# Two small cuts in a TensorE-bound transformer kernel: a PSUM tile of their own for four transposes, and smaller last pieces

## Chip, cores and metric

One core of one Trainium2 chip. The metric is the time of one execution in device microseconds. The span of a profile, from its first to its last instruction, is shorter than the time of the same execution: by about 1.7 us in 51 of the 60 executions for which both are known, by 1.9 to 2.9 us in the other nine. Figures with three decimals are starts or lengths of single instructions in the packed traces, called the records below; the views merge and round them.

## The reference

Four layers follow each other on x of 2048 tokens by 1024 features in bf16, twice this pair:

```python
x = x + A(layernorm(x))   # sliding dilated attention, 32 heads of 32, window 8, step 2; wqkv, wo
x = x + B(layernorm(x))   # gated MLP: (relu(x @ W_gate) * (x @ W_up)) @ W_down, 3584 hidden features
```

Nearly all of the work is matrix products. The kernel treats the tokens in blocks of 512, each of four tiles of 128 tokens.

## The kernel before

Only the first few microseconds and the last few matter here. All matmuls go through one helper (line 132), all VectorE (DVE) work of the first blocks through another (line 106), so in the profile the instructions are told apart by their tiles. PSUM is the memory in which the matmuls of this kernel leave their results, SBUF the one to which VectorE and ScalarE bring them; a bank of PSUM holds 512 fp32 columns here. `psum` is a pool of six one-bank accumulators, `psum_l` one tile of two banks.

The start: tile 0 of the tokens is normalised, transposed on TensorE (PE) and copied out of PSUM. Its projections on the value weights begin, and tile 1 follows with its transposes in two portions of four.

```python
def turn(t, halves=(0, 1)):
    ...
    elif t == 0:
        tps[t] = [psum.tile([P, KC // 2, P], BF16, tag="acc", name=f"tp{h}")[:] for h in range(2)]
    else:
        both = psum_l.tile([P, 2, KC, P], BF16, tag="L", name="tp_pair")
        tps[t] = [both[:, h, 0:KC // 2, :] for h in range(2)]
    for c in (h * (KC // 2) + i for h in halves for i in range(KC // 2)):
        with pe_group():
            tail_pe[0] = nc.tensor.transpose(tps[t][c // (KC // 2)][:, c % (KC // 2), :],
                                             xna[:, t, c * P:(c + 1) * P], ident[:]).ins
...
def second(h):
    turn(1, (h,))          # four transposes of tile 1
    copy(1, "v", h)        # PSUM -> SBUF on DVE, 512 columns
    ...
def head():
    for kc in range(KC // 2):
        for c in range(KC):
            if (kc, c) == (KC // 2 - 1, KC // 2):
                ln["second"](0)
            prod(kc, c, 0, 1)              # projections of tile 0, 128 columns each
    ln["second"](1)
# next on PE: prod(kc, c, 1, 2), tile 1's projections from the first copy
```

The end: the down projection of the last block of tokens, in two halves of 512 output columns. Each half sums 28 hidden chunks into accumulators, one for each piece of a tile, adds x on DVE, and stores.

```python
def cols_of(half):
    cols = [(t, 0, SLAB) for t in range(TPB)]
    if n == NN - 1 and half == 1:
        cols[-1:] = [(TPB - 1, 0, SLAB // 2), (TPB - 1, SLAB // 2, SLAB)]
    return cols
...
pair = psum_l.tile([P, TPB // 2, BLK], F32, tag="L", name="dacc_pair")
own = {2: pair[:, 0, :], 3: pair[:, 1, :]} if len(cols) == TPB else {2: pair[:, 0, :]}
accs[half] = [own[i] if i in own else psum.tile([P, BLK], F32, tag="acc", name=f"dacc{i}")[:]
              for i in range(len(cols))]
...
for a, (t, c0, c1) in zip(accs[half], cols):       # for each of four slabs of hidden chunks
    for jl in range(nfc):
        mm(a[:, c0:c1], lhsT=hT[:, j, t * P:(t + 1) * P], rhs=wsl[:, jl, c0:c1], ...)
...
for a, (t, c0, c1) in zip(accs[half], cols_of(half)):
    xs = x_tiles[b * TPB + t][:, half * SLAB + c0:half * SLAB + c1]
    run(nc.vector.tensor_tensor, xs, a[:, c0:c1], xs, op=ALU.add)
    ...  # store xs, on the SP or the ACT queue
```

## Time and profile before

The first three runs took 1617.74, 1617.75 and 1618.02 us.

The page of the profiled run: busy time by engine, then the chain of work that ended last.

```profile
span 1616.1 us, 18879 instructions
...
PE 1607.6 (99%) x7584; PEld 786.4 (49%) x7633; DVE 1138.5 (70%) x962; ACT 473.5 (29%) x964; POOL 180.3 (11%) x168
...
PE 99%; issue 0%; DMA 0%; DVE 0%; POOL 0%; ACT 0%; DVEq 0%
PE acc_u L132 24%; PE acc_g L132 24%; PE dacc L132 18%; PE acc_v L132 7%; PE acc_k L132 7%; PE acc_q L132 7%; PE acc_wo L132 7%; PE dacc_pair L132 6%; DMA x<-in_A_x_dram 0%; PE tp_pair L384 0%; DVE bst L103 0%; DVE bst L106 0%; POOL rstd L3
```

PE is busy for 99% of the span, and the chain is PE. The table of waits of PE over the whole program has three rows:

```profile
engine line waited for: us in total, times, longest us
PE scratch L132 <- DVE ones L309: 1.5, 1, 1.5
PE tp L384 <- DVE xn_first L106: 0.8, 1, 0.8
PE tp_pair L384 <- DVE xnT_first L106: 0.3, 1, 0.3
```

The first two are the start. The third is the one that the change aims at. The chain of waits around it (start, length, what; "issue" is time in which nothing is seen to be waited for):

```profile
8.99 0.28 PE acc_v L132 x5
9.27 0.36 PE tp_pair L384 x4
9.63 0.02 issue
9.66 0.44 DVE xnT_first L106
10.09 0.04 issue
10.13 0.38 PE tp_pair L384 x4
10.52 0.39 PE acc_v L132 x7
```

Four transposes of tile 1 are followed by the DVE copy of their result, then by the other four transposes, then by projections. In between PE has four projections of tile 0 (9.46 to 9.68 us), which are not on the chain. The second four transposes read nothing that the copy writes and write another bank. They wait because both portions lie in one tile, `tp_pair`, and the built program waits by tile.

The DVE timeline of the last microseconds (start, length, engine, line, operation, tiles, shape, count, and what ended the idle time before):

```profile
1610.45 0.69 DVE L838 TENSOR_TENSOR x<-dacc,x 128x512 bf16<-128x512 f32 x1 [20.95 <-PE dacc L132]
1611.31 0.69 DVE L838 TENSOR_TENSOR x<-dacc,x 128x512 bf16<-128x512 f32 x1 [0.17 <-PE dacc L132]
1612.18 0.69 DVE L838 TENSOR_TENSOR x<-dacc_pair,x 128x512 bf16<-128x512 f32 x1 [0.17 <-PE dacc_pair L132]
1612.78 0.74 DVE L838 TENSOR_TENSOR x<-dacc,x 128x256 bf16<-128x256 f32 x2
```

The adds of tiles 0 and 1 start 0.04 us after the last matmul of their accumulator. So does that of tile 2, at 1612.18. The two adds of tile 3 then follow in a row, at 1612.78 and, in the instruction's own record, 1613.115. The last store is issued at 1613.554 and the span ends 2.58 us after that.

### The profile page before, as it was taken

To read this page: it belongs to the slowest core of one execution; us is meant where nothing else is said; L and a number is where in the kernel's file an instruction comes from. 1 tells how busy PE (TensorE), PEld (TensorE's weight loads), DVE (VectorE), ACT (ScalarE), POOL (GpSimd) and SP (SyncE) were. 2 spreads that over 40 slices of the span, in tenths; PEclk is the share of its full clock that TensorE was granted. 3 is DMA by queue.
4 is the path that set the end of the run, shared out by engine and by line. 5 is a ranking of instruction groups with operands and counts; after the bars stand their busy time and mean duration, and the time that the engine had idled before them with its cause. 6 is when DMAs were issued, how large, how long until landed. Compare 5 with 4: busy or idle time off the path is not lost.

```text
span 1616.1 us, 18879 instructions
## 1 busy us (share of the span) xinstructions
PE 1607.6 (99%) x7584; PEld 786.4 (49%) x7633; DVE 1138.5 (70%) x962; ACT 473.5 (29%) x964; POOL 180.3 (11%) x168
## 2 busy tenths in 40 slices
PE   9999999999999999999999999999999999999999
PEld 6646544444444445444454444544445444444444
DVE  5999989996989698929389293893939939311211
ACT  4753312132115313603136031361313311131110
POOL 3400100010003002300053000530005100000000
PEclk9999999999999999999999999999999999999999
DMA  9767857596669666784747847489575884655452
GB/s 308 181 187 247 219 163 255 183 218 203 208 195 227 191 185 208 194 248 145 227 159 203 237 156 226 156 202 255 163 227 155 207 241 157 209 161 177 156 167 67
DMA packets 359064, 317.92 MB, mean 197 GB/s; under 512 B 105024, under 2 KB 332736, under 8 KB 358464
## 3 DMA queue, kind: packets, MB, share of 16 engines
q1 hardware_dynamic: 358272, 315.87, 67.1%
q8 instruction: 59, 0.97, 0.3%
q10 hardware_dynamic: 704, 0.85, 0.2%
q14 instruction: 29, 0.24, 0.0%
HBM read 266.29 MB, written 34.66 MB: 186 GB/s over the span
## 4 chain that ended last, share of the span: by engine, by line
PE 99%; issue 0%; DMA 0%; DVE 0%; POOL 0%; ACT 0%; DVEq 0%
PE acc_u L132 24%; PE acc_g L132 24%; PE dacc L132 18%; PE acc_v L132 7%; PE acc_k L132 7%; PE acc_q L132 7%; PE acc_wo L132 7%; PE dacc_pair L132 6%; DMA x<-in_A_x_dram 0%; PE tp_pair L384 0%; DVE bst L103 0%; DVE bst L106 0%; POOL rstd L327 0%; PE L L132 0%; DVE x L838 0%
## 5 line engine op out<-in xcount | busy, mean ns | idle before, releaser
L132 PE MATMUL acc_u<-xnT_b,w_u 128*128 128x512 bf16 x1792 | 423.3, 379 | 0.0
L132 PE MATMUL acc_g<-xnT_b,w_g 128*128 128x512 bf16 x1792 | 423.3, 379 | 0.0
L791 ACT ACTIVATE r<-acc_g 128x512 bf16<-128x512 f32 x224 | 133.6, 596 | 727.5 <-PE acc_g L132 696.8
L106 DVE TENSOR_TENSOR hT<-acc_u,r 128x512 bf16<-128x512 f32 x224 | 150.6, 685 | 241.2 <-PE acc_u L132 238.5
L132 PE MATMUL dacc<-w_d,hT 128*128 128x512 bf16 (+1 forms) x1372 | 300.4, 375 | 1.5
L132 PEld LDWEIGHTS <-hT 128*128 128x128 bf16 x1820 | 178.0, 98 | 209.0
L132 PEld LDWEIGHTS <-w_u 128*128 128x128 bf16 x1792 | 175.3, 98 | 211.4
L132 PEld LDWEIGHTS <-w_g 128*128 128x128 bf16 x1792 | 175.4, 98 | 211.4
L106 DVE TENSOR_TENSOR pv<-a,vhm 128x4096 bf16<-128x4096 bf16 x64 | 143.5, 2282 | 0.0
L838 DVE TENSOR_TENSOR x<-dacc,x 128x512 bf16<-128x512 f32 (+1 forms) x38 | 24.5, 672 | 154.2 <-PE dacc L132 154.2
L606 DVE TENSOR_TENSOR t<-q,k 128x2048 f32<-128x2048 bf16 x56 | 128.0, 2292 | 6.7 <-ACT k L541 4.6
L106 DVE TENSOR_TENSOR t<-q,k 128x2048 f32<-128x2048 bf16 x56 | 127.4, 2285 | 3.7 <-ACT k L541 2.6
L106 DVE TENSOR_TENSOR pv<-pv 128x1024 bf16<-128x1024 bf16 (+1 forms) x128 | 113.7, 949 | 0.0
L547 POOL COPY kh<-k 128x14 bf16<-128x14 bf16 x40 | 56.0, 1406 | 504.2 <-ACT k L541 504.2
L132 PE MATMUL acc_wo<-w_o,oT 128*128 128x512 bf16 x498 | 111.1, 379 | 0.7
L622 DVE TENSOR_TENSOR ac<-ac,t 128x2048 f32<-128x2048 f32 x48 | 109.6, 2284 | 0.3
L106 DVE TENSOR_TENSOR ac<-ac,t 128x2048 f32<-128x2048 f32 x48 | 109.6, 2283 | 0.0
L263 POOL TENSOR_TENSOR st_b<-st_b,neg_half 128x1 f32<-128x1 f32 x29 | 43.9, 1521 | 525.8 <-ACT st_b L262 525.8
L132 PE MATMUL dacc_pair<-w_d,hT 128*128 128x512 bf16 x413 | 95.5, 379 | 0.4
L132 PEld LDWEIGHTS <-oT 128*128 128x128 bf16 x512 | 50.2, 98 | 60.3
L258 ACT ACTIVATE xn_b<-x 128x1024 bf16<-128x1024 bf16 x29 | 30.3, 1045 | 129.3 <-DVE x L106 67.1
L444 ACT CAST vT<-acc_v 128x512 bf16<-128x512 f32 x56 | 32.6, 585 | 57.0 <-PE acc_v L132 56.1
(134 smaller groups left out, 1227.2 us busy)
## 6 DMA issues: line engine op xcount, KB each, us to landing
w_g<-in_B_W_gate_dram SPq DMA_DIRECT2D x56, 1024.0 KB, 7.1
w_u<-in_B_W_up_dram SPq DMA_DIRECT2D x56, 1024.0 KB, 5.4
w_d<-in_B_W_down_dram SPq DMA_DIRECT2D x48, 1024.0 KB, 5.9
w_o<-in_A_wo_dram SPq DMA_DIRECT2D x16, 1024.0 KB, 8.2
vhm<-v_d SPq DMA_DIRECT2D x32, 284.0 KB, 6.7
v_d<-vT SPq DMA_DIRECT2D x8, 1024.0 KB, 9.7
oT<-o_d SPq DMA_DIRECT2D x32, 256.0 KB, 3.4
w_d<-in_B_W_down_dram SPq DMA_DIRECT2D x16, 512.0 KB, 3.9
```

Source lines behind the costliest of these rows:

```text
L106: tail_dve[0] = f(*args, **kwargs).ins
L132: tail_pe[0] = nc.tensor.matmul(*args, **kwargs).ins
L258: nc.scalar.activation(xn, xt[:], ACT.Square, accum_out=sq)
L263: nc.gpsimd.tensor_tensor(rstd, vpe, neg_half[:, 0:1], op=ALU.pow)
L444: tail_act[0] = nc.scalar.copy(st["vT"][:, c, :], acc[:]).ins
L547: nc.gpsimd.tensor_copy(khalo[n][:, c, :], k[:, BLK:BLK + HALO])
L606: nc.vector.tensor_tensor(t[:], i0, i1, op=ALU.mult)
L622: nc.vector.tensor_tensor(o, i0, i1, op=ALU.add)
L791: tail_act[0] = nc.scalar.activation(rs[j][:], acc[:], ACT.Relu).ins
L838: run = dv if n < NB - 2 else (lambda f, *args, **kwargs: f(*args, **kwargs))
```

## The change

Intent: (1) let the second four transposes of tile 1 run during the copy, in a PSUM tile of their own; (2) let the last add and so the last store start earlier, by ending in smaller pieces: tile 2 in two pieces of 256 columns, tile 3 in 256, 128 and 128, with as many stores, of the same sizes, as before.

```diff
                 tps[t] = [both[:, h, 0:KC // 2, :] for h in range(2)]
+                if t == 1:
+                    tps[t][1] = psum.tile([P, KC // 2, P], BF16, tag="acc", name="tp_second")[:]
...
-                cols[-1:] = [(TPB - 1, 0, SLAB // 2), (TPB - 1, SLAB // 2, SLAB)]
+                cuts = [(TPB - 2, 0, 2), (TPB - 2, 2, 4), (TPB - 1, 0, 2), (TPB - 1, 2, 3), (TPB - 1, 3, 4)]
+                cols[-2:] = [(t, c0 * SLAB // 4, c1 * SLAB // 4) for t, c0, c1 in cuts]
...
-                        own = {2: pair[:, 0, :], 3: pair[:, 1, :]} if len(cols) == TPB else {2: pair[:, 0, :]}
+                        own = {2: pair[:, 0, :], 3: pair[:, 1, :]}
... (stores: tile 2 whole after its second piece; tile 3's first 256 columns, then its last 256 after the third piece)
```

With seven pieces, entries 2 and 3 of `own` are now the two pieces of tile 2.

## The prediction

> What bounds the kernel. The page gives TensorE (PE) 1607.6 of a 1616.1 us span, 99%, and the chain of waits is PE from end to end. The table of waits shows only three for PE: the first matmul on a memset (1.5 us), tile 0's transposes on the normalised x (0.8) and, at 10.1 us, tile 1's second four transposes on the VectorE (DVE) copy of the first four (0.3). After that PE never waits, so what is won at 10 us reaches the end, unless a load that is now just in time becomes late. What follows the last matmul (adds, last store, closing barrier) is the other exposed part.
>
> Head. In the timeline the four matmuls after the first transposes end their issue at 9.68; the second transposes start at 10.135, when the copy (9.656, 0.425 long) is done; the next projection matmul starts at 10.355. With a PSUM tile of their own the transposes run in that gap. But the projection matmul reads what the copy writes, so it now waits for the same copy and starts near 10.135. Gain: the four transposes, 4 x 55 ns = 0.22 us, and not the whole gap of 0.46. Loads have room: the second half of the value weights lands at about 10.1 and 11.5 us and is wanted from about 11.9. The extra buffer taken in the accumulator ring costs no wait that I can find.
>
> Tail, PE. Spacing in the trace: 512 columns 216 ns, 256 columns 109, 128 columns 56. Halving a matmul costs about 2.5 ns each time (the Trainium skill, "TensorE: Matmul & The Clock Gate", section "Wait — 56ns, not 53.3ns?", gives about 2.5 ns fixed per matmul; the trace agrees). Tile 2 is split once and tile 3 once more, for each of 28 hidden chunks: 56 x 2.5 = +0.14 us on PE.
>
> Tail, DVE. Before: the add of tile 2 (512 columns) starts at 1612.18, 0.04 after its last matmul; the next add follows 0.61 later, the last 0.33 after that, and takes 0.41; the last store is issued at 1613.55. The last two adds were already limited by DVE: the last piece's matmuls were done at 1613.01, its add began at 1613.115.
> After: both halves of tile 2 lie in one two-bank tile, and in the built program the first half's add waits for the last matmul of the second (the second add has no wait). So that split starts nothing earlier. DVE then runs in a row 256, 256, 256, 128, 128 columns: 3 x 0.33 + 0.20 (estimate: 0.33 less 128 columns at 1.08 ns, from 0.61 against 0.33 for 256 fewer) + 0.28 = 1.47 us, against 0.61 + 0.33 + 0.41 = 1.35.
>
> Sum at the last store's issue: -0.22 (head) + 0.13 (PE up to tile 2's end) + 0.12 (DVE) = +0.03 us. The number, queues and sizes of stores are the same, the last is still 64 KB, so landing (1.6 us) stays.
>
> Predicted: 1617.75 us, 1617.35 to 1618.15 (three runs of before already spread over 0.28). Faster by over 2%: 0.005; within 2%: 0.99; slower by over 2%: 0.005.
>
> What would show it. Head right: PE's wait at tile 1's transposes goes, a wait of the first tile-1 projection matmul for the copy appears, and that matmul starts 0.2 to 0.25 earlier. Tail right: the five adds run back to back from tile 2's last matmul, none of tile 2 starts before it, and the last store is issued within 0.1 us of 1613.55. Wrong if tile 2's first add starts about 0.44 earlier (then some 0.2 us are won), if 128-column matmuls cost more than 60 ns behind hidden-state weight loads (then a loss), or if the early gain is swallowed by a load before 25 us.

## The result

| | median | range | runs |
|---|---|---|---|
| before | 1618.12 | 1617.74 to 1618.83 | 6 |
| after | 1618.03 | 1617.73 to 1618.55 | 6 |

The ratio is 0.9999, interval 0.9986 to 1.0012. Here and below a ratio is the recorded one, from the fast runs of both kernels and with its 95% interval; it is not quite the ratio of the medians quoted. Executions over 1.5% slower than the fastest of the same kernel are left out of the means. The result is "the same", inside the predicted range.

The profiled run of after happened to be the slowest of its six:

```profile
span 1616.8 us, 19042 instructions
...
PE 1610.6 (100%) x7689; PEld 789.5 (49%) x7689; DVE 1138.9 (70%) x964; ACT 473.4 (29%) x964; POOL 180.5 (11%) x168
...
PE 99%; DMA 1%; DVE 0%; ACT 0%; issue 0%; POOL 0%; DVEq 0%; SPq 0%; ACTq 0%
PE acc_u L132 24%; PE acc_g L132 24%; PE dacc L132 18%; PE acc_v L132 7%; PE acc_q L132 7%; PE acc_wo L132 7%; PE acc_k L132 6%; PE dacc_pair L132 6%; DMA w_o<-in_A_wo_dram 1%; DMA x<-in_A_x_dram 0%; PE tp_pair L386 0%; DVE x L848 0%; DVE b
```

Its table of waits of PE:

```profile
engine line waited for: us in total, times, longest us
PE scratch L132 <- DVE ones L309: 1.5, 1, 1.5
PE tp L386 <- DVE xn_first L106: 0.6, 1, 0.6
PE acc_wo L132 <- DMA w_o<-in_A_wo_dram: 0.6, 1, 0.6
```

The wait at tile 1's transposes is gone, as intended. But a new one of 0.6 us stands in the output projection, `acc_wo` on the weights `w_o`. The chain around the former wait:

```profile
9.00 0.17 PE acc_v L132 x3
9.16 0.37 PE tp_pair L386 x4
9.53 0.02 issue
9.55 0.43 DVE xnT_first L106
9.99 0.04 issue
10.03 0.89 PE acc_v L132 x13
```

The chain now goes from the copy straight to the projections; the second transposes run beside it (from 9.58). PE is still held by the copy. The end, on DVE:

```profile
1611.01 0.69 DVE L848 TENSOR_TENSOR x<-dacc,x 128x512 bf16<-128x512 f32 x1 [21.07 <-PE dacc L132]
1611.87 0.69 DVE L848 TENSOR_TENSOR x<-dacc,x 128x512 bf16<-128x512 f32 x1 [0.17 <-PE dacc L132]
1612.74 0.76 DVE L848 TENSOR_TENSOR x<-dacc_pair,x 128x256 bf16<-128x256 f32 x2 [0.18 <-PE dacc_pair L132]
1613.42 0.81 DVE L848 TENSOR_TENSOR x<-dacc,x 128x256 bf16<-128x256 f32 x3
```

The add of tile 2 is now two adds in a row ("x2" at 1612.74). The first starts 0.87 us after the add of tile 1, as the single add did before, so the cut has started nothing earlier. Five adds run back to back where three did.

To take the run's luck out, I cut each trace at instructions that every version has, and use starts of single instructions:

- *start*: from the beginning to the first DVE copy of tile 1 out of PSUM,
- *head*: from there to the first query matmul,
- *middle*: from there to the first add of the last block's first half,
- *tail*: from there to the issue of the last store,
- *close*: from there to the end of the span.

| us | start | head | middle | tail | close | span |
|---|---|---|---|---|---|---|
| before | 9.66 | 13.939 | 1562.621 | 27.338 | 2.58 | 1616.13 |
| after | 9.55 | 13.714 | 1563.386 | 27.602 | 2.58 | 1616.83 |
| after minus before | -0.10 | -0.225 | +0.765 | +0.264 | 0.00 | +0.70 |

The change touches head and tail: -0.225 + 0.264 = +0.039 us, where the prediction had +0.03. The rest of the +0.70 is in stretches whose instructions are the same in both. The middle contains one gap in the matmuls that before has not, 0.755 us at 161.1 us, in front of `acc_wo` (0.971 from one start to the next, where the others are 0.216 apart). The experiments must tell whether the change brings that gap.

### The profile page after: what moved, and what is told of

The parts are those of the page before. It is cut to its first block, busy times and chain, and to the rows that moved or that the text cites. A ratio compares the mean times of both kernels' runs of the same rounds, so it can differ in the third digit from the quotient of the medians.

```text
span 1616.8 us, 19042 instructions
## 1 busy us (share of the span) xinstructions
PE 1610.6 (100%) x7689; PEld 789.5 (49%) x7689; DVE 1138.9 (70%) x964; ACT 473.4 (29%) x964; POOL 180.5 (11%) x168
## 4 chain that ended last, share of the span: by engine, by line
PE 99%; DMA 1%; DVE 0%; ACT 0%; issue 0%; POOL 0%; DVEq 0%; SPq 0%; ACTq 0%
PE acc_u L132 24%; PE acc_g L132 24%; PE dacc L132 18%; PE acc_v L132 7%; PE acc_q L132 7%; PE acc_wo L132 7%; PE acc_k L132 6%; PE dacc_pair L132 6%; DMA w_o<-in_A_wo_dram 1%; DMA x<-in_A_x_dram 0%; PE tp_pair L386 0%; DVE x L848 0%; DVE bst L103 0%; DVE bst L106 0%; ACT kst L540 0%
## 5 line engine op out<-in xcount | busy, mean ns | idle before, releaser
L132 PE MATMUL dacc<-w_d,hT 128*128 128x512 bf16 (+2 forms) x1428 | 302.0, 371 | 0.0
L132 PEld LDWEIGHTS <-hT 128*128 128x128 bf16 x1876 | 181.3, 98 | 206.0
L848 DVE TENSOR_TENSOR x<-dacc,x 128x512 bf16<-128x512 f32 (+2 forms) x39 | 24.5, 659 | 154.3 <-PE dacc L132 154.3
L132 PE MATMUL dacc_pair<-w_d,hT 128*128 128x512 bf16 (+1 forms) x448 | 95.9, 366 | 0.0
```

Source lines behind the costliest of these rows:

```text
L132: tail_pe[0] = nc.tensor.matmul(*args, **kwargs).ins
L848: run = dv if n < NB - 2 else (lambda f, *args, **kwargs: f(*args, **kwargs))
```

## The experiments

My theory: head and tail each do what was predicted and cancel; the gap of the middle is a load that came late by chance. The rivals: the earlier head makes the load late and so pays for itself there; and for the tail, that VectorE's number of adds matters whatever they wait for. Eight kernels were run; all gave correct results. The first four ran on one chip and share its nine runs of before (median 1617.82), the other four on another (median 1618.21).

| us | start | head | middle | tail | span | median (range; runs) |
|---|---|---|---|---|---|---|
| e1 head only | 9.74 | 13.713 | 1562.621 | 27.339 | 1616.00 | 1617.60 (1617.42 to 1617.94; 5) |
| e2 tail only | 9.96 | 13.938 | 1562.619 | 27.596 | 1616.69 | 1618.15 (1617.94 to 1618.58; 5) |
| e3 own tiles | 9.60 | 13.715 | 1562.620 | 27.373 | 1615.89 | 1617.57 (1617.48 to 1618.01; 5) |
| e4 late gate load | 9.44 | 13.938 | 1562.620 | 27.341 | 1615.91 | 1617.95 (1617.62 to 1618.85; 5) |
| e5 split copy | 9.54 | 13.582 | 1562.620 | 27.340 | 1615.67 | 1617.39 (1617.35 to 1618.95; 5) |
| e6 thin down | 9.92 | 13.937 | 1575.129 | 28.182 | 1629.71 | 1631.26 (1630.93 to 1631.60; 4) |
| e7 fine adds | 9.84 | 13.938 | 1562.620 | 28.175 | 1617.21 | 1619.68 (one run) |
| e8 change again | 9.47 | 13.715 | 1562.619 | 27.598 | 1616.00 | 1618.18 (1617.72 to 1618.30; 5) |

The record also has the span of every execution. Their means on the first chip are 1616.07 for before, 1615.92 for e1, 1616.52 for e2, 1615.94 for e3 and 1616.10 for e4; on the second 1616.43 for before, 1615.76 for e5 and 1616.38 for e8. They lean the way of the traces, but the start alone varies from 9.44 to 9.96 us in these profiles, so five runs do not fix a size.

### e1: only the transposes

```diff
+                if t == 1:
+                    tps[t][1] = psum.tile([P, KC // 2, P], BF16, tag="acc", name="tp_second")[:]
```

> Only the first half of the change: tile 1's second transposes in a PSUM tile of their own; the tail as before. Stretches read from the traces: first copy of tile 1 to first query matmul (head), first query matmul to the first add of the last block's first half (middle), that add to the issue of the last store (tail). Before they are 13.94, 1562.62 and 27.34 us, after 13.71, 1563.39 and 27.60. Theory (the two halves of the change cancel: head -0.22, tail +0.26; the 0.76 us of the middle is one late load of the output-projection weights that has nothing to do with the change): head 13.71, tail 27.34, and the middle 1562.6 plus whatever that load costs in this execution, so timed 0.2 us faster than before if enough executions are averaged. Rival (starting the matmuls earlier makes that load late, so the head gain is paid back there): middle 1563.0 or more here too, and no gain in time.

Measured: head 13.713, middle 1562.621, tail 27.339. The median is 1617.60 against 1617.82, ratio 0.9998 (0.9984 to 1.0012). The head gain is 0.226 us and all of it reaches the end: the projections start as much earlier as in after, but the middle has no gap. The rival falls for this execution. The difference of the medians, 0.22 us, has the expected size, but the interval of the ratio is far wider than that, so the times do not establish it.

### e2: only the tail

```diff
-                cols[-1:] = [(TPB - 1, 0, SLAB // 2), (TPB - 1, SLAB // 2, SLAB)]
+                cuts = [(TPB - 2, 0, 2), (TPB - 2, 2, 4), (TPB - 1, 0, 2), (TPB - 1, 2, 3), (TPB - 1, 3, 4)]
+                cols[-2:] = [(t, c0 * SLAB // 4, c1 * SLAB // 4) for t, c0, c1 in cuts]
... (own and the stores as in the change)
```

> Only the second half of the change: the tail cut as in the change, tile 1's transposes as before. Theory: head 13.94, tail 27.60 (0.14 of the 0.26 us on TensorE, 56 extra matmul starts of 2.5 ns; 0.12 on VectorE, three adds of 256 and two of 128 columns in a row where there were 512, 256, 256); timed about 0.25 us slower than before, at the edge of what five rounds can show. Rival for the late load (the head's earlier start causes it): here the head is not early, so no stall in the middle: 1562.6. Under the theory of chance the stall can appear here too.

Measured: head 13.938, tail 27.596, ratio 1.0002 (0.9989 to 1.0014), median 1618.15 against 1617.82. Within the tail, the add of tile 2 starts 26.089 us after the stretch's beginning (25.960 before, so PE costs 0.13 us up to there), and from that start to the last store are 1.507 us (1.378 before, so DVE costs 0.13 us). So by the traces this half of the change is a loss of 0.26 us, and it hides the gain of the other. (How the 0.26 us splits is tried in e3, e6 and e7.)

### e3: tile 2's pieces in accumulators of their own

```diff
-                        own = {2: pair[:, 0, :], 3: pair[:, 1, :]}
+                        own = {2: pair[:, 0, :], 3: pair[:, 1, :]} if len(cols) == TPB else {6: pair[:, 0, :]}
```

> The change, but tile 2's two halves in accumulators of their own instead of the two halves of one two-bank tile (the last 128 columns of tile 3 get the two-bank tile). Theory (the first half's add waits for the second half's matmuls because they share a tile, so the cut of tile 2 buys nothing): here tile 2's first add starts when the add of tile 1 lets it, about 0.61 us after that add started instead of 0.87; the last add is then limited by TensorE again and not by a row of adds, and the tail is 27.37 (27.35 to 27.42) instead of 27.60. Rival (VectorE is limited by the number of adds whatever they wait for): tail stays 27.55 or more.

Measured: tail 27.373 against 27.60. The DVE timeline:

```profile
1610.28 0.69 DVE L848 TENSOR_TENSOR x<-dacc,x 128x512 bf16<-128x512 f32 x1 [21.07 <-PE dacc L132]
1611.15 1.93 DVE L848 TENSOR_TENSOR x<-dacc,x 128x512 bf16<-128x512 f32 x5 [0.17 <-PE dacc L132]
1613.00 0.28 DVE L848 TENSOR_TENSOR x<-dacc_pair,x 128x128 bf16<-128x128 f32 x1
```

Five adds now follow the one of tile 1 in a row from 1611.15: tile 1 whole, two of tile 2, the first two of tile 3. In the records tile 2's first add starts 0.607 us after tile 1's, as soon as DVE is free, where it started 0.87 us after it in the change. The tail falls by 0.23 us though pieces, adds and stores are the same in number and size: so the wait of tile 2's first add for the matmuls of the second, through the shared two-bank tile, is what lost that time. The rival falls. Yet the tail is only back at the level of before (27.34): the cuts cost PE 0.14 us (the modelled end of the last matmul is 26.935 us into the tail, in before 26.796), so even with separate tiles this cut wins nothing; other cuts were not tried. One detail of the expectation is wrong: the last add is not limited by PE. It starts 0.13 us after the end of its matmuls, at the end of a row of three adds; it is the first add of that row, tile 3's first piece, that waits for PE (0.037 us after its last matmul). Times: median 1617.57 against 1617.82, ratio 0.9998 (0.9986 to 1.0011).

### e4: another load moved away from the late one

```diff
-            events.append((ends[i - RING] + 0.3 if i >= RING else 0.1 * i, lambda ...: load_slab(key, src)))
+            at = ends[i - RING] + 0.3 if i >= RING else 0.1 * i
+            at = t_wo0 + 4.0 if key == ("g", 0, 0) else at
+            events.append((at, lambda ...: load_slab(key, src)))
```

> The kernel before with one load moved: the first 1 MB of gate weights, issued at about 152 us although it is first read at 190, is issued some 12 us later, after the output-projection weights that are read from 160 us on. Theory (those two loads and the query and key stores share the queues, and the output-projection load, 8.6 us to landing before and 10.1 after, is sometimes too late): it lands in 6 us or less, no stall of the output projection in any execution, middle 1562.6, and the spread of the times of this kernel is smaller than that of the kernel before (1617.74 to 1618.83), near its low end: 1617.7 to 1617.9. Rival (the spread comes from elsewhere, or the stall is a matter of when the load is issued): median and spread as before.

The DMA issues between 142 and 158 us (out<-in, queue, count, size, us from issue to landing) of before, of after, and of e4:

```profile
w_o<-in_A_wo_dram SPq DMA_DIRECT2D x1, 1024.0 KB, 8.6
w_g<-in_B_W_gate_dram SPq DMA_DIRECT2D x1, 1024.0 KB, 10.8
```

```profile
w_o<-in_A_wo_dram SPq DMA_DIRECT2D x1, 1024.0 KB, 10.1
w_g<-in_B_W_gate_dram SPq DMA_DIRECT2D x1, 1024.0 KB, 12.2
```

```profile
w_o<-in_A_wo_dram SPq DMA_DIRECT2D x1, 1024.0 KB, 9.2
```

My expectation failed. Without the gate weights behind it the load took 9.2 us, longer than in before, and the times spread as before (1617.62 to 1618.85 against 1617.55 to 1618.48; the spans, which leave out the 2.55 us by which the 1618.85 exceeds its own, 1615.9 to 1616.3 against 1615.8 to 1616.6). So moving that load did not bring this one in early. That it has no part in the delay is not shown: with it gone, the stores of the keys (`k_d`) were issued from 152.70 us on and not from 157.27, so other transfers took its place. What the ten profiles do show is the margin. In before the load is issued at 151.29 us and the matmul that reads it starts about 9.4 us later; in after, the issue is at 150.97 us and, without the stop, the reader would have started 9.4 us later too: the change moves both alike, so it does not shorten the time that the load has. The load took 7.5, 7.9, 8.4, 8.5, 8.6, 8.7, 8.8, 8.9 and 9.2 us in nine profiles, and 10.1 in the profile of after, where PE stopped. Why it takes 7.5 us once and 10.1 another time stays open.

### e5: the copy cut in two

```diff
... (tile 1's second transposes in a tile of their own, as in e1)
-            copy(1, "v", h)
-            if h == 0:
-                return
+            if h == 0:
+                copy(1, "v", h, 0, KC // 4)
+                copy(1, "v", h, KC // 4, KC // 2)
+                return
+            copy(1, "v", h)
... (first_half, for t == 1: for kc outside, for c inside; tail as before)
```

> The head of the change, the tail of before, and the first copy of tile 1 cut in two of 256 columns, with tile 1's first projections ordered so that the first eight need only the first piece. In e1 the projections still wait for the whole copy: TensorE has nothing to do from 9.80 to 10.03 us in the profile of after. Theory (what is left of the gap is the copy's length, 0.43 us, less the transposes): the first piece takes about 0.29 us, the projections start about 0.15 us earlier and find the second piece done; head 13.55 (13.50 to 13.62) against 13.71 in e1 and 13.94 before, middle 1562.62, tail 27.34; about 0.4 us faster than before in time. Rival (another wait, the transposes themselves or the second piece, ends at the same time): head 13.68 or more.

Measured: head 13.582. The chain of waits:

```profile
9.15 0.35 PE tp_pair L386 x4
9.51 0.22 PE acc_v L132 x4
9.73 0.22 PE tp_second L386 x4
9.95 0.99 PE acc_v L132 x16
```

In this view the chain goes from PE to PE, but it counts with modelled ends of matmuls, which overlap. The records say more. The last of the transposes starts at 9.732, so at their spacing of 0.056 us the projections could have followed at 9.79. The first piece of the copy takes 0.292 us from 9.542, and the projections start at 9.887, 0.345 us after the copy's start (0.478 in after). That is 0.053 us after the end of the first piece, and in after they start 0.053 us after the end of the whole copy: PE still waits for the copy, only for a shorter one. So of the 0.233 us that the change had left on the table in the head, shortening the copy wins 0.133, and 0.10 remain behind its first piece. Head gain against before: 0.357 us; middle and tail are unchanged, so all of it reaches the end. Four of its five runs lie at 1617.35 to 1617.43, below all nine of before, and one at 1618.95 (its span is 1616.1, so 2.85 us lie outside it, where the other four have 1.7); ratio 0.9996 (0.9984 to 1.0009). By the traces it is the best version tried; by the times it is not shown to be faster.

### e6: all down matmuls cut to 128 columns

```diff
-                            mm(a[:, c0:c1], lhsT=hT[:, j, t * P:(t + 1) * P], rhs=wsl[:, jl, c0:c1],
-                               start=(j == 0), stop=(j == FC - 1))
+                            for m0 in range(c0, c1, P):
+                                mm(a[:, m0:m0 + P], lhsT=hT[:, j, t * P:(t + 1) * P], rhs=wsl[:, jl, m0:m0 + P],
+                                   start=(j == 0 and m0 == c0), stop=(j == FC - 1 and m0 + P == c1),
+                                   skip_group_check=True)
```

> The kernel before with every matmul of the down projections cut into four of 128 columns in the same accumulator (adds and stores as before): 1792 matmuls become 7168. It enlarges the one suspected cost of the tail's TensorE part. Theory (a cut costs the fixed 2.5 ns per matmul and nothing else, also with a weight load per 128 columns): 7.4 ns per former 512-column matmul, +13 us, 1630 to 1632. Rival (the Trainium skill, TensorE: Matmul & The Clock Gate, section Back-to-back issue gap, gives about 81 ns for 128 columns in a stream of weight loads and matmuls): 108 ns per former matmul, +190 us.

Measured: 1631.26 us, ratio 1.0080 (1.0064 to 1.0095). Middle and tail together grow by 12.51 + 0.84 = 13.35 us. The groups of matmuls by shape (busy time, mean ns of one, idle before):

```profile
L132 PE MATMUL dacc<-w_d,hT 128*128 128x128 bf16 x5488 | 312.1, 219 | 0.0
L132 PE MATMUL dacc_pair<-w_d,hT 128*128 128x128 bf16 x1680 | 99.0, 219 | 0.0
```

13.35 us over 1792 former matmuls of 512 columns is 7.45 ns for each, so (216 + 7.45) / 4 = 55.9 ns for one of 128 columns, with a weight load in front of each (28 of the 1792 were in two pieces already, which changes little); the records have 55 or 56 ns from start to start. The theory stands, and the cost of a cut on PE is measured enlarged: about 2.5 ns. (The lengths of single matmuls in the fence, 219 ns, overlap; it is their spacing that counts.)

### e7: the same adds in 16 pieces

```diff
-                    run(nc.vector.tensor_tensor, xs, a[:, c0:c1], xs, op=ALU.add)
+                    step = 64 if n == NN - 1 and half == 1 and t >= 2 else SLAB
+                    for m0 in range(0, c1 - c0, step):
+                        m1 = min(m0 + step, c1 - c0)
+                        run(nc.vector.tensor_tensor, xs[:, m0:m1], a[:, c0 + m0:c0 + m1], xs[:, m0:m1], op=ALU.add)
```

> The kernel before with the last three adds (512, 256, 256 columns) done in 16 adds of 64 columns, the matmuls and stores as before. It enlarges the suspected VectorE part of the tail. Theory (an add costs a fixed 0.06 to 0.07 us besides its columns, and the row of adds after tile 2's last matmul is what the last store waits for): 13 more adds, +0.8 us; tail 28.15 (28.05 to 28.3) against 27.34. Rival (only columns count, or the last store waits for TensorE): tail under 27.6.

Measured: tail 28.175 against 27.338, +0.837 us for 13 more adds, 0.064 us each. The DVE timeline:

```profile
1611.49 0.69 DVE L838 TENSOR_TENSOR x<-dacc,x 128x512 bf16<-128x512 f32 x1 [0.17 <-PE dacc L132]
1612.35 1.14 DVE L838 TENSOR_TENSOR x<-dacc_pair,x 128x64 bf16<-128x64 f32 x8 [0.17 <-PE dacc_pair L132]
1613.41 1.13 DVE L838 TENSOR_TENSOR x<-dacc,x 128x64 bf16<-128x64 f32 x8
```

From 1612.35 to the end DVE does nothing but adds, 0.131 us from one start to the next. All of their cost is in the tail, so the last store does wait for the row of adds, and not for PE.

### e8: the change once more

The edit is the whole change.

> The change once more, for a second profile of it. Theory (the stall of 0.76 us in the output projection was one late load by chance, as it came in one of six profiles so far and not in e1 and e3, which start as early): head 13.71, middle 1562.62, tail 27.60, span about 1616.1 to 1616.4; timed within 0.2 us of before. Rival (head and tail together bring the stall): middle 1563.3 again.

Measured: head 13.715, middle 1562.619, tail 27.598, span 1616.00; median 1618.18 against 1618.21, ratio 0.9999 (0.9986 to 1.0011). The gap of the middle did not come back. It appeared in one of the two profiles of the change and in none of the eight of the other versions, before among them; e1, e3 and e5 are as early and have none. The early head is therefore not sufficient for it. That it would never happen to the kernel before is not shown.

## Why the prediction was right

- *PE bounds the kernel and never waits after the first 10 us.* Right for every trace but one. The middle is 1562.619 to 1562.621 us in eight of the nine profiles whose middle has the same matmuls; in the first profile of after PE waited once more, 0.755 us, for a load. The prediction named a late load as a risk, but placed it before 25 us and blamed the early start; the run-to-run spread of a load with 0.2 to 1.9 us to spare was not seen.
- *Head, -0.22 us: the four transposes, not the whole gap.* Measured -0.225 (after), -0.226 (e1), -0.224 (e8). The projection matmuls wait for the same copy; e5 shortens that wait to half of the copy and gets 0.13 us more.
- *Tail on PE, +0.13 us up to tile 2's end.* Measured +0.131 (26.091 against 25.960). The step rests on the Trainium skill, "TensorE: Matmul & The Clock Gate", section "Wait — 56ns, not 53.3ns?", about 2.5 ns fixed for each matmul; this agrees: 216, 109 and 56 ns from start to start for 512, 256 and 128 columns, and 2.5 ns for each cut in e6.
- *Tail on DVE, +0.12 us: the cut of tile 2 starts nothing earlier.* Measured +0.133. e3 shows the reason given: with separate tiles the first add starts 0.61 us after tile 1's and not 0.87. The Trainium skill, "PSUM — Partial Sum Buffer", section "PSUM bank collisions raise a hardware error", asks for guards by bank and quadrant; the two pieces lie in two banks, and e3 gives correct results without that wait, so the wait came from the tile and not from the memory.
- *Sum +0.03 us.* Measured +0.039 in the first profile, +0.036 in e8. The times cannot confirm it: the range of 0.4 us to either side would have held as well if neither half had done anything. That the sum is right for the reasons given is read from the stretches and from e1, e2 and e3.
- *One sign was badly chosen.* "The last store is issued within 0.1 us of 1613.55" failed as written: 1614.26 in the first profile, 1613.40 in the second, because load and start differ from execution to execution. The sign should have been a distance inside the tail.

## What to carry to other kernels

A cut into smaller pieces only starts something earlier if each piece can be waited for alone: look in the built program at what the first consumer waits for, and give the pieces tiles of their own. Price both sides before cutting, the producer's fixed cost times all its repetitions (here 28 chunks for one add) and the consumer's fixed cost at the end; here, in e3, they ate all of the gain. And when effects are a tenth of the run-to-run spread, cut the traces at common instructions and compare stretches, not times or absolute moments.

## What the Trainium skill lacked or had wrong

- "TensorE: Matmul & The Clock Gate", section "Back-to-back issue gap", gives about 81 ns per matmul of 128 columns in a stream of weight loads and matmuls. In e6, 7168 such matmuls of 128 columns, each with its weight load, took 55.9 ns each, about the figure that the page calls isolated.
- The same page, section "What's actually happening", lets the clock rise after about 3.4 us of activity. Here the dummy matmuls at the start went from 427 to 216 ns apart after 2.9 us in before, and in e2 all 13 stayed at about 427 ns, up to the first transpose, which came 5.5 us after the first of them and was delayed by them (7.04 us against 6.69 in before), as e2's chain of waits shows (its ends are modelled):

```profile
1.52 5.73 PE scratch L132 x13
7.25 0.28 PE tp L384 x4
```

  The page does say that the window runs freely; a warm-up of fixed length must allow for both.
- "VectorE: DVE Perf Modes", section "The TRN2 errata", gives 120 cycles plus the columns for a PSUM source. The length of one add of 512 columns is 0.691 us as the page's formula for an fp32 add has it. But adds in a row follow each other after 0.331 us for 256 columns, 0.198 for 128 and 0.131 for 64 (after, e7), that is, by an estimate with the page's clock of 0.96 GHz, some 62 cycles plus the columns: it is this spacing that prices a row, and that section does not give it for a PSUM source.
- No page that I found says how much the landing time of one and the same load varies between executions: 1 MB took 7.5 to 10.1 us here, on a queue with other loads and stores.
